# Load releases in a fused linear-attention and feed-forward kernel: fewer warm-up matmuls, weight and chunk loads tied to products

## The chip, the cores and the metric

The kernel runs on one core of one Trainium2 chip. The metric is the device time of one execution in microseconds; the figure given for a kernel is the median of its runs. Lower is better.

## The reference, cut to what matters

There are 4 batches, 8 heads, 768 positions and a head width of 64. The first half is linear attention with a decay per head, worked in blocks; the second half is a feed-forward layer with a "snake" activation over the 3072 tokens that come out of it.

```python
intra = einsum(q_block, k_block) * Dmask          # decay inside the block
out   = einsum(intra, v_block) + einsum(q_block * lam_pow, state)
state = lam_block * state + einsum(k_block * rev_pow, v_block)
...
h = x @ w_in                                      # 3072x512 by 512x2048
g = h + sin(alpha * h)**2 / (alpha + 1e-9)
y = g @ w_out                                     # 2048x512
```

## The kernel before, in words

**Attention steps.** Tokens are handled in 24 steps. A pair of batches, a block of 128 positions and a half of the heads make one step `s`; two steps share one load `d` (`d = s // 2`), so there are 12 loads each of q, k and v. q and k are cast to bf16 by their transfers[...]; v arrives as f32. `load(d, x)` (L298) issues two transfers, one for each batch of the pair; with `by_step=True` it issues four, one for each batch and half of the heads, so that a step can start on half of the data. For each step, `sec()` (L433) puts up to three pieces on TensorE (PE): the transposes of q and k (`t=`, L444), the scores (`s=`, L453) and the outputs together with the new state (`o=`, L466, L476, L489). Behind them, `prep_v` (L416, instruction L423) scales v by a decay table and casts it, `put_S` (L559) masks the scores on VectorE (DVE), and `put_O` (L571) writes the result transposed into `xT` (L581, DVE), copies the state `Zs` (L591 on ScalarE, called ACT, or L604 on GpSimd, called POOL) and keeps the running state `Zacc` (L586, L602). A step `o` needs its scaled v, its masked scores and the `Zs` of step `o-2`.

**Chunks.** Four steps give one chunk `c` of 512 tokens; there are six chunks. For each chunk, 16 groups `grp_A(c, m)` (L632, matmuls L640) form the first product, 128 columns of `w_in` each. A group is four matmuls of 128x512, and after it come a sine on ACT (L644), a square on whichever engine would end first (L649 to L653) and one combining instruction on DVE (L654) into `gT`. The second product is `grp_B(c, s4, m4)` (L669, matmuls L677): four 128-token tiles in four steps of four matmuls each. A finished tile is copied out by ACT (L684) and stored by two transfers on the SP queue (L690). "GEMM1 of chunk 1" below means the 16 groups `grp_A(1, 0..15)`; "the second product of chunk 0" means the `grp_B(0, ...)` that run just before them, with the attention steps 4 to 7 between them.

**Weights.** `w_in` comes in four blocks of four column groups (`w1_block`, L405, issue at L408) and `w_out` in four blocks (`w2_block`, L411, issue at L413), all cast to bf16 on the POOL queue.

**What sets the order.** Nothing in the program is issued in the order in which it is written. `Program.add` (L86) is a planner: each operation has an assumed duration, and `place` and `probe` (L65, L75) put it at the earliest time at which its inputs are ready and its engine has a gap. PE and SP keep the written order (they only have a `free` time); DVE, ACT and POOL can be back-filled. A transfer is planned from its issue cost (`ISSUE`, L35), one shared transfer rate (`RATE`), a start delay (`BEGIN`) and an end delay (`DONE`), L36, L107 to L114. A load on POOL is never placed before the load that was recorded ahead of it (`self.issued`, L109), but otherwise it goes as early as its buffer allows. The instructions are then emitted sorted by planned start (L117), with semaphore waits where one engine needs another. On the chip, each engine's queue runs strictly in this order. So the planned durations decide orders and engine choices (`fastest`, L284), and the real durations decide the time. An `after=` list adds dependencies by hand.

**The start.** L715 to L760 write the first four steps by hand. `idle_pe(32)` (L379) runs 32 matmuls on a zeroed tile; nothing reads them. The POOL queue gets, in this order, the loads of k, q for `d=0` and `d=1`, small constants, eight transfers for v (`d=0` and `d=1`, `by_step`), the first block of `w_in`, a small constant (L353), the four `prep_v` of steps 0 to 3, and the other three blocks of `w_in`. The first group of GEMM1 needs `xT` of steps 0 to 3.

**The loads of later chunks.** `ISSUE_A0`, `ISSUE_B0` and `ISSUE_A1` (L788 to L790) say after which group a load is recorded, not when it is issued. A load of chunk 2 (`d=4`, `d=5`) has a free buffer long before it is recorded, so the planner can back-fill it behind the load recorded before it. `ahead` (L764) records the `prep_v` of later steps and the loads `d` from 6 on.

Of the kernel before, what the change touches and what calls it, by code (L numbers as in the profile page):

```python
# [27 lines left out]
class Program:  # L28
# [4 lines left out]

    ENGINES = ("PE", "DVE", "ACT", "POOL", "SP")
    ISSUE = {"SP": 0.66, "POOL": 0.75, "ACT": 0.66}  # L35
    HOP, RATE, BEGIN, DONE = 0.1, 190e3, 1.6, 1.0  # L36

    def __init__(self):
        self.ops = []
# [46 lines left out]
    def add(self, eng, fn, dur, reads=(), writes=(), slot=None, nbytes=0, after=()):  # L86
        op = Op(eng, fn, dur, len(self.ops))
        self.ops.append(op)
        op.deps = self.deps_of(reads, writes) | set(after)
        for b in reads:  # L90
            if b.startswith("b."):
                op.deps.update(r for r in self.readers.get(b, ()) if r.eng != eng)
        for b in reads:
            self.readers.setdefault(b, []).append(op)
        for b in writes:
            self.writer[b] = op
            self.readers[b] = []
        op.nbytes = nbytes
        t = self.ready(eng, op.deps)
        if slot is None:  # L100
            op.start = self.place(eng, t, dur)
            op.end = op.start + dur
            return op
        op.slot = slot
        self.slots[slot] = self.slots.get(slot, 0) + 1
        op.kslot = self.slots[slot]
        issue = self.ISSUE[eng] * (0.6 if 10000 < nbytes < 100000 and eng == "POOL" else 1)  # L107
        op.start = self.place(eng, max(t, self.issued[eng]), issue)
        self.issued[eng] = op.start  # L109
        if nbytes < 10000:  # L110
            op.end = op.start + 2.9
        else:
            self.dma_free = max(self.dma_free, op.start + self.BEGIN) + nbytes / self.RATE
            op.end = self.dma_free + self.DONE  # L114
        return op
# [72 lines left out]
def bass_lightning_attn__then__act_snake_kernel(  # L188
# [10 lines left out]
    B, H, S, D = q.shape  # L199
# [20 lines left out]
    with es:  # L220
# [50 lines left out]
        P = Program()  # L271
# [26 lines left out]
        def load(d, x, after=(), by_step=False, eng=None):  # L298
            pair, n = d // NB, d % NB
            r = d % RL  # L300
            src, dst = {"k": (k, k2), "q": (q, q2), "v": (v, v32)}[x]
            ops = []
            for h0, h1 in ((0, HS), (HS, H)) if by_step else ((0, H),):
                for u in range(2):
                    a = bass.AP(src.tensor, ((2 * pair + u) * H + h0) * S * D + n * BL * D,
                                [[2 * D, 64], [S * D, h1 - h0], [1, 2 * D]])
                    keys = [f"{x}.{r}.{u}.{h // HS}" for h in range(h0, h1, HS)]
                    op = rec(eng or ("SP" if x == "v" else "POOL"),
                             lambda e, u=u, a=a, h0=h0, h1=h1: e.dma_start(dst[r][half(u), h0:h1, :], a), 0,  # L309
                             writes=keys, slot=f"{x}{r}{h0 if by_step else ''}{'p' if eng else ''}",  # L310
                             nbytes=(216500 if x == "v" and eng is None else 166000) * (h1 - h0) // H, after=after)
                ops.append(op)
            return ops if by_step else op

# [398 lines left out]
                        reads=[f"ol.{z}"], slot=f"ol{z}{t}", nbytes=64 * 1024)  # L713

        load(0, "k")  # L715
        q0 = load(0, "q")
        consts()
        idle_pe(32)
        iotas()
        consts3()  # L720
        load(1, "k")
# [2 lines left out]
        sec(t=0, tb=(0, 1), t_engs=("DVE",))  # L724
        sec(t=1, tb=(2, 3), t_engs=("ACT",))
        consts2()
        load(0, "v", by_step=True, eng="POOL")
        load(1, "v", by_step=True, eng="POOL")
        w1_block(0, 4)
        identf_op()  # L730
        decay_table(0, 2)
        sec(s=0, sb_=4)
        sec(t=2, tb=(0, 1), t_engs=("DVE",))
        sec(s=1, sb_=6)
        sec(t=3, tb=(2, 3), t_engs=("ACT",))
        decay_table(2, NB)
        prep_v(0, ("POOL",))
        prep_v(1, ("POOL",))
        sec(s=2, sb_=0)
        zl = []  # L740
        s3 = sec(s=3, sb_=2, via=True, later=True)
        sec(o=0, ob=4, z_late=zl)
        s3()
        prep_v(2, ("POOL",))
        prep_v(3, ("POOL",))
        sec(o=1, ob=6, z_late=zl)
        w1_block(4, 4)
        w1_block(8, 4)
        w1_block(12, 4)
        o2 = sec(o=2, ob=0, later=True)  # L750
# [27 lines left out]
            b = pick_bank(range(4)) if t is not None else 0  # L778
            return sec(t=t, o=o, s=s, tb=(b, b), peek=peek, x_first=i % 4 == 3)

        def loads(*what):
            for x, d in what:
                if x == "w":
                    w2_block(4 * d, 4)
                else:
                    load(d, x, eng="POOL" if d < 4 else None)

        ISSUE_A0 = {0: [("w", 0)], 2: [("k", 2)], 4: [("q", 2)], 6: [("w", 1)], 9: [("k", 3)], 12: [("q", 3)]}  # L788
        ISSUE_B0 = {0: [("v", 2), ("w", 2)], 2: [("v", 3), ("w", 3)], 8: [("k", 4)], 10: [("q", 4)]}
        ISSUE_A1 = {0: [("v", 4)], 1: [("k", 5)], 3: [("q", 5)], 4: [("v", 5)]}  # L790
        AHEAD_A1 = {8: 8, 11: 9, 14: 10}
        LAST_B0 = {1: (2, 3), 3: (3, 3)}
        every, low = range(8), range(4)
# [5 lines left out]
        SQ = {3: "ACT", 6: "DVE", 8: "ACT", 11: "DVE", 13: "ACT"}  # L799
        for c in range(NCH):  # L800
            for m in range(NM):
                grp_A(c, m, every if m < 12 else range(2, 4) if m == 15 and c else range(4, 8),
                      (SQ.get(m, "POOL"),) if c > 1 else ("POOL", "ACT", "DVE"))
                if c < 2:
                    loads(*(ISSUE_A0, ISSUE_A1)[c].get(m, ()))
                if c == 1 and m in AHEAD_A1:
                    ahead(AHEAD_A1[m])
                if c == 1 and m in LAST_B0:
# [58 lines left out]
```

## Time and profile before

| What | Value |
|---|---|
| median of 6 runs | 230.0 us (228.82 to 232.35) |
| the profiled execution, its own time | 229.39 us |
| its span from the first to the last instruction | 227.2 us |
| PE busy in the span | 207.5 us, 91% |
| DVE, ACT, POOL busy | 141.8, 125.0, 121.8 us |
| mean granted clock of PE | 0.960 |
| first group of GEMM1 of chunk 0 | from about 21.6 us |
| second product of chunk 0, with steps 4 to 7 | about 37 to 59.6 us |
| GEMM1 of chunk 1 | about 59.6 to 76 us |

All times inside the span count from its start. "PEld" is the loading of a stationary operand, which runs beside PE. In lists of waits, "<-issue" means that an engine stood still although nothing that the profile shows held it. In the list of transfers, q0 is the queue that POOL issues to, q1 the one that SP issues to, and q8 carries instructions to the engines.

### The profile page before, as it was taken

The page shows a single profiled execution, that of the slowest core. Times are in us where ns is not written, and L with a number is a line of the kernel's source. Part 1 is how long each engine was busy: PE and PEld are TensorE (multiplying, and loading weights), DVE is VectorE, ACT ScalarE, POOL GpSimd, SP SyncE. Part 2 cuts the span into 40 slices and gives each one's busy share as a digit, 9 for nine tenths or more (in the row PEclk, how much of TensorE's full clock was granted, in tenths as well). Part 3 has the DMA queues.
Part 4 walks back from the last instruction along what each step waited for, and adds up shares of the span by engine and source line. Part 5 has one row for each costly group of instructions (what it writes and reads, how often), then busy time and mean ns, then how long its engine had stood idle before and what let it go on. Part 6 is the DMA issues. An engine that isn't in the chain of part 4 may idle for free.

```text
span 227.2 us, 6426 instructions
## 1 busy us (share of the span) xinstructions
PE 207.5 (91%) x2800; PEld 109.9 (48%) x2833; DVE 141.8 (62%) x201; ACT 125.0 (55%) x194; POOL 121.8 (54%) x160
## 2 busy tenths in 40 slices
PE   6377999986999899999999999999999999999994
PEld 5255444453444455544455544455544554444453
DVE  2768599464579955658747487855478664378400
ACT  4835699130499734577636577533677432568130
POOL 8997999325603516685626587533364500555300
PEclk9655899999999999999999999999999999999999
DMA  7988999999999606990509942503200204102043
GB/s 67 154 194 124 206 179 193 243 196 144 130 187 283 127 3 93 194 137 0 133 8 120 234 48 23 139 3 88 58 0 3 48 3 95 46 0 48 1 92 92
DMA packets 42923, 23.49 MB, mean 103 GB/s; under 512 B 26880, under 2 KB 39440, under 8 KB 42896
## 3 DMA queue, kind: packets, MB, share of 16 engines
q0 software_dynamic: 30272, 12.59, 44.2%
q1 hardware_dynamic: 12368, 10.42, 18.8%
q8 instruction: 22, 0.36, 0.6%
q10 hardware_dynamic: 256, 0.08, 0.2%
q14 instruction: 5, 0.04, 0.1%
HBM read 27.28 MB, written 6.29 MB: 148 GB/s over the span
## 4 chain that ended last, share of the span: by engine, by line
PE 81%; DVE 7%; POOL 6%; issue 4%; ACT 1%; POOLq 0%
PE PS L640 33%; PE PS L677 32%; PE PS L444 5%; DVE gT L654 3%; PE PS L466 3%; PE PS L476 3%; PE PS L453 2%; POOL v L309 2%; PE PS L704 2%; PE PS L489 1%; DVE u L652 1%; POOL k L309 1%; POOL q L309 1%; DVE S_m L568 1%; DVE xT L581 1%
## 5 line engine op out<-in xcount | busy, mean ns | idle before, releaser
L640 PE MATMUL PS<-xT,w 128*128 128x512 bf16 x376 | 86.8, 383 | 1.3 <-DVE Zacc L602 1.0
L677 PE MATMUL PS<-w,gT 128*128 128x512 bf16 x343 | 82.0, 379 | 3.8 <-issue 3.6
L654 DVE SCALAR_TENSOR_TENSOR gT<-u,r_sb,PS 128x512 bf16<-128x512 bf16 x96 | 69.7, 746 | 24.7 <-POOL u L652 21.8
L644 ACT ACTIVATE t<-PS,alpha_sb 128x512 bf16<-128x512 f32 x96 | 63.4, 682 | 21.5 <-PE PS L640 21.3
L652 POOL TENSOR_TENSOR u<-t 128x512 bf16<-128x512 bf16 x44 | 45.3, 1049 | 31.5 <-ACT t L644 31.4
L640 PEld LDWEIGHTS PS<-xT,w 128*128 128x128 bf16 x384 | 37.3, 99 | 47.7 <-issue 2.5
L677 PEld LDWEIGHTS PS<-w,gT 128*128 128x128 bf16 x368 | 33.9, 98 | 39.6
L568 DVE TENSOR_TENSOR S_m<-PS,mask 128x1024 bf16<-128x1024 f32 x23 | 28.0, 1222 | 22.8 <-PE PS L453 22.8
L623 ACT COPY qkT<-PS 128x1024 bf16<-128x1024 bf16 x21 | 21.2, 1011 | 29.4 <-PE PS L476 18.9
L423 POOL TENSOR_TENSOR v<-v,Lv 128x512 bf16<-128x512 f32 x20 | 20.9, 1059 | 30.1 <-DMA v<-in_v_dram 15.9
L684 ACT COPY osb<-PS 128x512 f32<-128x512 f32 x23 | 13.5, 585 | 31.4 <-PE PS L677 31.4
L581 DVE TENSOR_TENSOR xT<-PS,Xt 128x512 bf16<-128x512 f32 x24 | 16.3, 684 | 12.9 <-PE PS L476 11.9
L309 POOL DMA_DIRECT2D k<-in_k_dram x24 | 17.3, 745 | 8.7 <-PE PS L476 4.9
L444 PE MATMUL PS<-ident,q 64*64 64x64 bf16 x384 | 14.3, 205 | 6.2 <-DMA q<-in_q_dram 5.1
L651 ACT ACTIVATE u<-t 128x512 bf16<-128x512 bf16 x28 | 17.6, 630 | 1.4
L604 POOL CAST Zs<-Zacc 128x256 bf16<-128x256 f32 x16 | 6.8, 428 | 20.0 <-DVE Zacc L602 20.0
L444 PEld LDWEIGHTS PS<-ident,q 64*64 64x64 bf16 x384 | 9.7, 114 | 15.9 <-issue 11.0
L309 POOL DMA_DIRECT2D q<-in_q_dram x24 | 17.1, 743 | 0.0
L652 DVE TENSOR_TENSOR u<-t 128x512 bf16<-128x512 bf16 x24 | 14.2, 592 | 3.2 <-ACT t L644 3.2
L476 PE MATMUL PS<-qkT,Zs 64*64 64x128 bf16 x160 | 15.6, 232 | 0.4
L466 PE MATMUL PS<-S_m,v 64*64 64x128 bf16 x384 | 14.2, 235 | 1.1 <-POOL v L423 0.7
L444 PE MATMUL PS<-ident,k 64*64 64x64 bf16 x384 | 13.5, 200 | 0.0
(50 smaller groups left out, 131.8 us busy)
## 6 DMA issues: line engine op xcount, KB each, us to landing
out_dram<-osb SPq DMA_DIRECT2D x46, 128.0 KB, 3.0
v<-in_v_dram SPq DMA_DIRECT2D x16, 256.0 KB, 6.4
k<-in_k_dram POOLq DMA_DIRECT2D x24, 128.0 KB, 5.7
q<-in_q_dram POOLq DMA_DIRECT2D x24, 128.0 KB, 6.5
w<-in_moe_w_in_dram POOLq DMA_DIRECT2D x4, 512.0 KB, 7.4
w<-in_moe_w_out_dram POOLq DMA_DIRECT2D x4, 512.0 KB, 13.1
v<-in_v_dram POOLq DMA_DIRECT2D x8, 128.0 KB, 3.5
v<-in_v_dram POOLq DMA_DIRECT2D x4, 256.0 KB, 13.9
```

The lines of the kernel that those rows point to most:

```text
L309: lambda e, u=u, a=a, h0=h0, h1=h1: e.dma_start(dst[r][half(u), h0:h1, :], a), 0,
L423: rec(eng, lambda e: e.tensor_tensor(v2[c][:, :, :], src, L_b, ALU.mult), dur, reads=reads, writes=writes)
L444: last = e.transpose(dst, part((q2, k2)[x], t, u, h, tt), ident[half(u), half(u)])
L466: return e.matmul(dst, v2[o % RC][half(u), hid(h, tj), :], S_m[o % RS][half(u), h % 2 ^ u, h // 2, tj, :], start=start, stop=True, skip_gr ...
L476: return e.matmul(dst, Zs[(o - 2) % 3][half(r), u, h // 2, :], qkT[o % RQ][half(r), u, 0, h // 2, :], start=start, stop=True, skip_group_c ...
L568: rec("DVE", lambda e: e.tensor_tensor(s_out, s_in, mask_b, ALU.mult), 1.25, reads=keys_s + ["mask.0", "mask.1"], writes=[f"S_m.{s % RS}"])
L623: rec(eng, lambda e: (e.copy if eng == "ACT" else e.tensor_copy)(to, ti), dur, reads=keys_t, writes=[f"qkT.{j}"])
L640: last = e.matmul(PS[:, i, :], w1[:, kc, 128 * m:128 * (m + 1)], xT[x][:, kc, :], start=(kc == 0), stop=(kc == NKC - 1))
L644: rec("ACT", lambda e: e.activation(t16[tt][:, :], PS[:, i, :], ACTF.Sin, scale=alpha_sb[:, m:m + 1]), 0.7, reads=bk(i) + ["alpha"], write ...
L652: return e.tensor_tensor(u16[tt][:, :], t16[tt][:, :], t16[tt][:, :], ALU.mult)
L654: rec("DVE", lambda e: e.scalar_tensor_tensor(out=gT[g][:, m, :], in0=u16[tt][:, :], scalar=r_sb[:, m:m + 1], in1=PS[:, i, :], op0=ALU.mul ...
L677: last = e.matmul(PS[:, bank, :], gT[g][:, m, 128 * s4:128 * (s4 + 1)], w2[:, m, :], start=(m == 0), stop=(m == NM - 1))
```

## The change

- The planner's constants: `BEGIN` 1.6 to 1.5, `DONE` 1.0 to 1.2, the issue cost of mid-sized POOL transfers, and the assumed sizes of q, k and v transfers.
- 16 zero matmuls in place of 32.
- v for `d=1` is loaded by two transfers in place of four.
- Scores of step 1 are recorded ahead of the transposes of step 2; outputs of step 0 are recorded ahead of the scores of step 3.
- The second block of `w_in` is recorded right after the outputs of step 0, and waits for them (`after=[P.ops[-1]]`, the PE piece of `o=0`); the scalings of v for steps 2 and 3 are recorded behind it. The third and fourth block stay behind those.
- The loads of k and q for `d=4` move from the second product of chunk 0 to GEMM1 of chunk 1. Every load recorded in GEMM1 of chunk 1 (k, q, v of `d=4` and `d=5`) waits for the PE piece of the group after which it is recorded.

```diff
-    HOP, RATE, BEGIN, DONE = 0.1, 190e3, 1.6, 1.0
+    HOP, RATE, BEGIN, DONE = 0.1, 190e3, 1.5, 1.2
...
-        issue = self.ISSUE[eng] * (0.6 if 10000 < nbytes < 100000 and eng == "POOL" else 1)
+        issue = self.ISSUE[eng] * (0.85 if 10000 < nbytes < 100000 and eng == "POOL" else 1)
...
-                             nbytes=(216500 if x == "v" and eng is None else 166000) * (h1 - h0) // H, after=after)
+                             nbytes=(187000 if d < 2 else 150000) if x != "v" else 216500 // (2 if by_step else 1), after=after)
...
-        idle_pe(32)
+        idle_pe(16)
...
-        load(0, "v", by_step=True, eng="POOL")
-        load(1, "v", by_step=True, eng="POOL")
+        load(0, "v", eng="POOL", by_step=True)
+        load(1, "v", eng="POOL")
         w1_block(0, 4)
         identf_op()
         decay_table(0, 2)
         sec(s=0, sb_=4)
+        sec(s=1, sb_=6)
         sec(t=2, tb=(0, 1), t_engs=("DVE",))
-        sec(s=1, sb_=6)
         sec(t=3, tb=(2, 3), t_engs=("ACT",))
         decay_table(2, NB)
         prep_v(0, ("POOL",))
         prep_v(1, ("POOL",))
+        zl = []
         sec(s=2, sb_=0)
-        zl = []
-        s3 = sec(s=3, sb_=2, via=True, later=True)
-        sec(o=0, ob=4, z_late=zl)
-        s3()
+        o0 = sec(o=0, ob=4, z_late=zl, later=True)
+        w1_block(4, 4, after=[P.ops[-1]])
+        sec(s=3, sb_=2, via=True)
+        o0()
+        sec(o=1, ob=6, z_late=zl)
         prep_v(2, ("POOL",))
         prep_v(3, ("POOL",))
-        sec(o=1, ob=6, z_late=zl)
-        w1_block(4, 4)
         w1_block(8, 4)
         w1_block(12, 4)
...
-        def loads(*what):
+        def loads(*what, after=()):
...
-                    load(d, x, eng="POOL" if d < 4 else None)
+                    load(d, x, eng="POOL" if d < 4 else None, after=after)
...
-        ISSUE_B0 = {0: [("v", 2), ("w", 2)], 2: [("v", 3), ("w", 3)], 8: [("k", 4)], 10: [("q", 4)]}
-        ISSUE_A1 = {0: [("v", 4)], 1: [("k", 5)], 3: [("q", 5)], 4: [("v", 5)]}
+        ISSUE_B0 = {0: [("v", 2), ("w", 2)], 2: [("v", 3), ("w", 3)]}
+        ISSUE_A1 = {1: [("k", 4)], 2: [("q", 4), ("v", 4)], 4: [("k", 5)], 5: [("q", 5), ("v", 5)]}
...
-                grp_A(c, m, every if m < 12 else range(2, 4) if m == 15 and c else range(4, 8),
+                op = grp_A(c, m, every if m < 12 else range(2, 4) if m == 15 and c else range(4, 8),
...
-                    loads(*(ISSUE_A0, ISSUE_A1)[c].get(m, ()))
+                    loads(*(ISSUE_A0, ISSUE_A1)[c].get(m, ()), after=[op] if c else [])
```

## The prediction

> **What bounds the kernel now.** I read the 40 slices of the page first, then the chain of work that ended last over the start, then the gaps of PE in the list in order of time, and last the transfer queues around the largest gap.
>
> ```profile
> PE   6377999986999899999999999999999999999994
> PEclk9655899999999999999999999999999999999999
> DMA  7988999999999606990509942503200204102043
> ```
>
> After the fourth slice (22 us) PE is full, but for the ninth and tenth (45 to 57 us) and, less, the fourteenth. So a microsecond is to be had in the first 22 us, in the 50s, or nowhere: elsewhere an earlier load finds PE busy anyway. The start, by the chain:
>
> ```profile
> 9.25 4.17 POOL v L309 x7
> ...
> 13.51 0.87 POOL w L408
> ...
> 14.48 1.03 POOL v L423
> 15.56 0.64 PE PS L466 x16
> ...
> 20.88 0.69 DVE xT L581
> ```
>
> POOL's queue sets it: eight v transfers, the first `w_in` block, a constant, then the scaling that step 0's outputs wait for. The end of the start is the `xT` of step 3 at 21.57 us; GEMM1 follows. The hole in the 50s, by PE's list in order of time:
>
> ```profile
> 51.52 0.22 PE L476 MATMUL PS<-qkT,Zs 64*64 64x128 bf16 x2
> 53.37 0.33 PE L489 MATMUL PS<-v,k 64*64 64x64 bf16 x12 [1.63 <-issue]
> ```
>
> PE stops 1.63 us in the middle of one emitted piece, step 5's outputs, where no semaphore wait can stand.[...] What is left is that its instructions were not there. Two views speak for that. Busy times with instruction counts, from zero to the end of the hole and from zero to 47.07 us:
>
> ```profile
> 0.00:53.36 53.36, 41.29 (x722) 25.01 (x729) 35.48 (x53) 29.60 (x50) 41.29 (x66) 0.84 1.20 173
> 0.00:47.07 47.07, 37.21 (x596) 22.46 (x602) 31.27 (x48) 28.59 (x49) 39.46 (x64) 0.82 1.15 171
> ```
>
> PE and PEld together: 1451 against 1198, 253 apart. The page's queue q8 has 22 instruction packets of 0.36 MB for 5633 PE and PEld instructions, 256 per packet of 16 KB. So the block that was missing at 53.37 could be asked for when the one before the last was used up, at about 47.07. The queues at the one packet near it (window 50.9 to 51.1 us):
>
> ```profile
> q0 software_dynamic: 141, 0.04, 178.0%
> q8 instruction: 1, 0.02, 29.6%
> ```
>
> It left only at 51.00, 3.9 us after 47.07, while POOL's transfers (q0) filled the 16 engines. At about 80 us, with q0 empty, the same step two blocks on took 0.9 us, from 79.98 to 80.85. What fills q0 then:
>
> ```profile
> 33.54 0.91 POOL L413 DMA_DIRECT2D w<-in_moe_w_out_dram  x1
> 34.30 1.53 POOL L309 DMA_DIRECT2D k<-in_k_dram  x2
> 35.65 1.53 POOL L309 DMA_DIRECT2D q<-in_q_dram  x2
> 36.99 1.56 POOL L309 DMA_DIRECT2D k<-in_k_dram  x2
> 38.32 1.58 POOL L309 DMA_DIRECT2D q<-in_q_dram  x2
> ```
>
> These k and q are `d=4` and `d=5`, chunk 2, back-filled to 34 us although nothing needs them before 76 us. Their landing times in the transfer view are 16.7 to 17.4 us (51.0 to 55.7); the last `w_out` block lands at 33.54 + 17.1 = 50.6.
>
> **The change, part by part.**
>
> *Zero matmuls.* The 32 take 3.47 us (1.17 to 4.64). The Trainium skill (TensorE: Matmul & The Clock Gate, "Part 1: The HAM clock gate") says that some 3.4 us of sustained work release the clock; 16 matmuls, 1.73 us, would by that not release it, and the rule speaks against halving them. If the release reached the start's work, 9.36 us of PE at half rate, losing it could cost up to 4.7 us (half of it). But the rows say that it reaches nothing:
>
> ```profile
> 4.64:8.20 3.56, 0.00 (x1) 0.00 (x1) 2.61 (x5) 2.10 (x6) 3.56 (x7) 0.94 1.34 127
> 8.20:21.60 13.40, 9.36 (x337) 7.57 (x337) 10.07 (x13) 8.16 (x14) 12.53 (x19) 0.50 0.95 159
> ```
>
> PE idles until q lands at 8.2, and from there its clock is 0.50 with all 32 in place. I take 0. A side effect: 32 fewer PE instructions (16 and their weight loads) move each block end 32 instructions later in the program.
>
> *v in six transfers.* Eight cost 4.99 us on POOL, 0.62 each. Now 4 x 0.62 + 2 x 0.74 (row of `d=2`: 1.48 a pair) = 3.98: `w_in`, the constant and the first scalings come 1.01 us earlier, step 0's outputs at 14.55 in place of 15.56. Scaling 2 now needs all of `d=1`; the last of its small transfers landed at 12.9 + 3.3 = 16.2, and the new ones are issued by 12.6, so it is there at about 16.
>
> *Second `w_in` block.* It waits for step 0's outputs (to 15.41), is issued at 15.5 for 0.80 us, and behind it in POOL's queue stand scalings 2 and 3, then blocks three and four. So scaling 2 ends at 17.33 (17.49 before), scaling 3 at 18.33 (18.49). Of the 1.01 us, 0.85 is spent here. Step 3's masking is the other gate of step 3:
>
> ```profile
> 17.10 1.94 DVE L565 TENSOR_TENSOR S_m<-S_raw,mask 128x1024 bf16<-128x1024 bf16 x1
> ```
>
> It ends at 19.04, 0.55 after POOL's last scaling, though begun at 17.10. Step 3's scores now run after step 0's outputs (15.4 to 16.0), ACT copies them in 1.01, so it begins at 17.05, again under scaling 3: it ends at 18.9. Then 2.5 us to GEMM1 as before. The start gains 0.15 us. Bounds: 1.0 gained if the masking gets in ahead of scaling 3 and everything moves by POOL's 1.01; 0.6 lost if `d=1` lands that much later. The early block itself lands before 22, where it was needed at 27: hidden. If GEMM1 ever waited for it, its issue at 15.5 in place of 18.44 would be worth 2.9 us.
>
> *Step 1's scores first.* They fit into PE's wait for q of `d=1` (10.8 to 11.85): 0. Their masking (1.22) delays a DVE copy by 0.26, hidden behind the scalings. *Planner constants.* They reorder, they cost nothing alone. ACT's sine table (1.28 + 0.20 at 20.07) fits into a planned gap behind the decay tables, as the planner now has the copy of step 3 later; ACT is not in the chain there: 0.
>
> *Chunk 2's loads.* Eight POOL issues leave 34 to 40 us, where POOL then waits idle: 0. The loads of `d=6`, `d=7` move with them, since no load passes the one ahead. The fetch for the block that ends in the hole is now asked for at 47.5 and its code needed at 52.4 (32 instructions on, without the hole). From the last `w_out` block q0 is empty, at 50.6 or earlier: the `w_in` blocks start sooner, into the 18 to 20 us slot where only 53 GB/s moved, which takes up to 2 us off the queue, so at about 49. Fetch 49.0, packet 0.95, and from the packet to PE's restart before 53.37 - 51.95 = 1.42: code at 51.4, or at 53.0 with 50.6. That is a stall of 0 to 0.6 us in place of 1.63; I take 0.3, a gain of 1.3. Bounds: 0 (the fetch's lag is that of `w_out`, not of chunk 2) and 1.63. The skill's Runtime: NRT & Kernel Launch, "Instruction fetch mechanics", has the fetch of 256 instructions mostly hidden; by that rule the hole is something else, the gain 0 and the sum 229.4. The row, 253 instructions and a late packet, is nearer; I go by it.
>
> In GEMM1 of chunk 1 the eight issues (1.36 to 1.53 a pair) stand on POOL from 61.5 to 68.6, each pair held until a group ends. Behind them are the scalings of steps 8 and 9 (70.5 before) and nothing else. POOL was idle from 63 to 70.5, and that hides 5.7 us of issue; without it the scalings would slip toward 82, where step 8 is used. SP: v of `d=4` moves behind two stores (63.34, 0.92 each), from 61.5 to about 65.2, v of `d=5` from 67.1 to 68.8, `d=6` to 70.7. Landing in 7 us, v4 is there at 72 and scaled by 74; needed at 82.3: hidden. k, q of `d=4` have 12 us to 76: hidden. But transfers crowd 62 to 84 now, 4.2 MB and the stores at 175 to 250 GB/s, 22 us. Two blocks fetched at 80 and 86 have 5.3 and 4.4 us: lost 0 to 1.6, taken 0.2, since the queue thins by then.
>
> *Sum* against the profiled execution: 229.39 - 0.15 - 1.3 + 0.2 = 228.1. The median of the runs is 0.6 above that execution: **228.7**.
>
> **Rivals.**
>
> *The hole only moves.* q0 is still full of `w_out` at 47.5, or the later crowd holds up the fetch at 86 as it did at 47. Then 230.0 - 0.15 to + 0.3: 229.8 to 230.3. For: 3.6 us of lag at 44.37 already, with chunk 2 hardly moving. Against: the packet left within 0.4 us of `w_out`'s landing.
>
> *The start gives all of its 1.01.* For: POOL leads the chain from 8.7 to 15.5. Against: the masking's 1.94. 228.7 - 0.9 = 227.8.
>
> *Slower: a scaling on DVE waits for v of `d=6`.* The planner gives a scaling to the engine that ends first, and at step 12's scaling it now sees this v later than before, when DVE has a gap, at about 82. DVE's queue is in order: behind it is the masking of step 9 (83.50). From a landing at 82.8 on, each microsecond of lateness goes to PE. Issued at 70.7 and landing in 6.6 to 7.2 us it comes at 78; with the longest v landing of the trace, 15.9, at 86.6, and 3.8 are lost: 228.7 + 3.8 = 232.5.
>
> **How the numbers follow.** Hole filled, start unchanged 0.52 (228.7, its own range 227.5 to 229.7); hole moves 0.20; start gains 0.15; slower 0.13. About 1% is what a measurement of this kernel can tell from no change: below 227.7, above 232.3. Faster: half of the start's case, a quarter of the first: 0.22. Slower: the DVE case and a tenth of the moved hole: 0.15. Same 0.63. Range 226.8 to 231.5.
>
> **What would show it.** Right: chunk 2's k and q at 61 to 69 us; no PE gap over 0.6 in 45 to 57; GEMM1 from 21.3 to 21.7; clock 0.5 from 8 us on as before. Wrong: GEMM1 from 20.7 (the start counted), a gap in 85 to 91 (fetch), an idle DVE at 82 to 87 ahead of L423 (v6), PE's clock at half for longer than 25 us.

## The result, and the profile after

| | kernel before | kernel after |
|---|---|---|
| median of the runs | 230.52 us (70 runs) | 231.47 us (228.75 to 234.18, 33 runs) |
| ratio after/before | | 1.003, 95% interval 1.0007 to 1.0054 |
| the profiled execution, its own time | 229.39 us | 230.43 us |
| its span | 227.17 us | 228.22 us |

The change makes the kernel a little slower; the forecast was 228.7 us, 0.6% faster. (Ratios here and below leave disturbed runs out; in group C of the experiments that leaves only 16 of 75 runs of the kernel before, so there the medians of all runs are read as well.)

The two profiled executions differ by 1.05 us of span. Taking from each trace the start of the first group of GEMM1 of chunk 0, of the second product of chunk 0, and of GEMM1 of chunks 1 and 2 gives the place of each part:

| stage | before | after | difference |
|---|---|---|---|
| to GEMM1 of chunk 0 | 21.62 | 22.46 | +0.84 |
| GEMM1 of chunk 0 | 15.19 | 16.01 | +0.82 |
| second product of chunk 0 and steps 4 to 7 | 22.74 | 21.54 | -1.20 |
| GEMM1 and second product of chunk 1 | 35.43 | 35.97 | +0.54 |
| the rest | 132.19 | 132.24 | +0.05 |

So the expected gain is there, in the third stage, and three others give it back. (How much of that belongs to the change, and how much to this pair of executions, is told below.) The page of the changed kernel, 40 slices again:

```profile
PE   3465999998999998999999999999999999999994
PEclk9999999999999999999999999999999999999999
DMA  6999999960399999990418952604200204101043
```

The row PEclk does not mean full speed in the start. The first clock record of this trace is at 26.56 us, and a stretch without a record reads 1.00; the spacing of the matmuls shows half rate until then (the first two groups of GEMM1 take 1.26 and 1.71 us, as in the kernel before, and 0.86 later).

The dip of PE in the ninth and tenth slice is gone (9 and 8 instead of 8 and 6). The new one is small, in the sixteenth slice (86 to 91 us), where the kernel before had a 9. In DMA, the ninth to eleventh slice have emptied (9, 9, 9 to 6, 0, 3) and the fourteenth and fifteenth, 74 to 86 us, have filled up (6 and 0 to 9 and 9). The gaps of PE in the order of time that are longer than 0.4 us, behind the first group of GEMM1:

```profile
54.46 1.90 PE L677 MATMUL PS<-w,gT 128*128 128x512 bf16 x7 [0.41 <-issue]
...
86.83 0.21 PE L444 MATMUL PS<-ident,k 64*64 64x64 bf16 x1 [0.77 <-issue]
```

The hole that was 1.63 us at 53.37 is 0.41 us, behind step 5's outputs in place of in the middle of them. The one at 86.83 is new, again in the middle of an emitted piece, where no semaphore wait can stand.

**The second late block.** PE and PEld had used up a block of 256 instructions at about 80.1 us, and the next packet of q8 left at 84.33. The transfer queues around it (84.2 to 84.5 us; packets, MB, and the summed time of the packets as a share of the 16 engines, which can be above 100%):

```profile
q0 software_dynamic: 192, 0.05, 161.1%
q8 instruction: 1, 0.02, 18.6%
```

4.2 us from request to packet, with q0 full: the lag that was 3.9 us at 47 to 51 in the kernel before. In the kernel before, the transfers were done by then. Busy time and DMA share in three stretches, before and then after (the last three columns are granted clock, DMA share and GB/s):

```profile
80.00:85.00 5.00, 4.68 (x133) 2.90 (x130) 2.72 (x3) 2.03 (x2) 1.04 (x1) 1.00 0.01 3
85.00:90.00 5.00, 4.58 (x129) 2.57 (x130) 3.40 (x6) 2.19 (x3) 2.87 (x6) 1.00 0.45 76
```

```profile
80.00:85.00 5.00, 4.68 (x130) 2.83 (x126) 2.79 (x3) 2.02 (x2) 2.68 (x3) 1.00 1.51 205
85.00:90.00 5.00, 3.77 (x99) 2.27 (x99) 2.68 (x6) 2.18 (x3) 1.93 (x4) 1.00 0.98 128
```

PE loses 0.81 us of busy time in the second stretch (4.58 to 3.77).

**The start.** POOL's list in order of time:

```profile
13.69 2.04 POOL L423 TENSOR_TENSOR v<-v,Lv 128x512 bf16<-128x512 f32 x2 [0.27 <-DMA v<-in_v_dram]
15.98 0.80 POOL L408 DMA_DIRECT2D w<-in_moe_w_in_dram  x1 [0.25 <-PE PS L489]
17.43 2.32 POOL L423 TENSOR_TENSOR v<-v,Lv 128x512 bf16<-128x512 f32 x2 [0.66 <-DMA v<-in_v_dram]
19.71 1.55 POOL L408 DMA_DIRECT2D w<-in_moe_w_in_dram  x2
```

POOL came to the scaling of step 2 at 16.8 us and waited 0.66 us for v of `d=1`. The masking of step 3, which the prediction took for the second gate, began in that wait and ended at 17.85, long before POOL's last scaling (19.75):

```profile
17.16 0.69 DVE L565 TENSOR_TENSOR S_m<-S_raw,mask 128x1024 bf16<-128x1024 bf16 x1 [0.75 <-ACT S_raw L564]
```

It had been 1.94 us long when POOL was scaling as it began. Here it began first, and POOL's scaling of step 2, begun within it, took 1.32 us in place of 1.03. So in this execution v, not the masking, set the end of the start.

**GEMM1 of chunk 0.** The kernel before has an uninterrupted run of groups to its end. The changed one, where PE's list breaks:

```profile
28.80 6.21 PE L640 MATMUL PS<-xT,w 128*128 128x512 bf16 x28
35.22 3.63 PE L640 MATMUL PS<-xT,w 128*128 128x512 bf16 x15 [0.21 <-DVE gT L654]
```

A matmul waits for DVE's combining instruction of an earlier group. What the line L640 waited for between 33 and 38 us, and who waited for L654 in that time (us, times):

```profile
  DVE gT L654: 0.8, 3
...
  PEld PS L640: 0.6, 2
  PE PS L640: 0.2, 1
```

From the starts of the groups' first weight loads, groups 11 to 14 are 1.42, 0.68, 1.08 and 0.76 us long, 3.94 together, where the kernel before has four times 0.86, 3.44: 0.50 us. The rest of that stage's 0.82 is mostly the clock: PE's full rate came 4.10 us after the stage's start (26.56) in place of 3.24 (24.86), and until then a group takes 1.71 us in place of 0.86, which is some 0.4 us.

The banks are the planner's doing. `pick_bank` (L281) takes the PSUM bank that is free first in the plan. Groups 0 to 11 may use all eight, groups 12 to 15 only four (banks 4 to 7). The two plans give groups 0 to 15 these banks:

```
before: 5 6 7 0 1 4 2 3 5 6 7 0 4 5 6 7
after:  5 6 7 4 0 1 2 3 5 6 7 4 5 6 7 4
```

In the new plan the sine table (L389) stands earlier in the start, at 10.96 in place of 17.96 us of planned time. The copy that reads bank 4 no longer stands behind it, and bank 4 looks free before bank 0 (20.59 and 21.23; in the plan of before 19.76 and 19.58). So group 3 takes bank 4, and group 11 again. The new constants alone (e8) and the new start alone (e7) give the same banks. Group 12 then has to take bank 5, which group 8 left only four groups ago; before, it had bank 4, untouched since group 5.

### The profile page after: what moved, and what is told of

Same layout as the page of the kernel before. It is cut to its first block, busy times and chain, and to the rows that moved or that the text cites. A ratio compares the mean times of both kernels' runs of the same rounds, so it can differ in the third digit from the quotient of the medians.

```text
span 228.2 us, 6391 instructions
## 1 busy us (share of the span) xinstructions
PE 206.2 (90%) x2784; PEld 107.8 (47%) x2817; DVE 139.8 (61%) x201; ACT 124.9 (55%) x194; POOL 121.0 (53%) x158
## 4 chain that ended last, share of the span: by engine, by line
PE 84%; DVE 4%; POOL 4%; issue 4%; DMA 2%; ACT 1%; POOLq 0%; DVEq 0%
PE PS L640 34%; PE PS L677 34%; PE PS L444 5%; PE PS L466 3%; PE PS L476 3%; PE PS L453 3%; DVE gT L654 2%; DMA v<-in_v_dram 2%; PE PS L704 2%; POOL k L309 1%; POOL q L309 1%; PE PS L489 1%; DVE xT L581 1%; DVE S_m L568 1%; POOL v L423 0%
## 5 line engine op out<-in xcount | busy, mean ns | idle before, releaser
L640 PE MATMUL PS<-xT,w 128*128 128x512 bf16 x376 | 87.5, 385 | 1.6 <-DVE Zacc L602 1.0
L677 PE MATMUL PS<-w,gT 128*128 128x512 bf16 x343 | 81.9, 379 | 4.2 <-issue 4.1
L654 DVE SCALAR_TENSOR_TENSOR gT<-u,r_sb,PS 128x512 bf16<-128x512 bf16 x96 | 69.8, 746 | 24.8 <-POOL u L652 21.5
L640 PEld LDWEIGHTS PS<-xT,w 128*128 128x128 bf16 x384 | 37.2, 99 | 48.6 <-issue 3.7
L677 PEld LDWEIGHTS PS<-w,gT 128*128 128x128 bf16 x368 | 33.9, 98 | 40.1 <-issue 0.6
L423 POOL TENSOR_TENSOR v<-v,Lv 128x512 bf16<-128x512 f32 x20 | 21.0, 1063 | 24.6 <-DMA v<-in_v_dram 15.5
L444 PE MATMUL PS<-ident,q 64*64 64x64 bf16 x384 | 14.3, 205 | 5.7 <-POOL ident L316 5.0
L444 PEld LDWEIGHTS PS<-ident,q 64*64 64x64 bf16 x384 | 9.6, 114 | 15.5 <-issue 7.2
L652 DVE TENSOR_TENSOR u<-t 128x512 bf16<-128x512 bf16 x24 | 13.4, 557 | 4.1 <-ACT t L644 4.1
L444 PE MATMUL PS<-ident,k 64*64 64x64 bf16 x384 | 13.7, 200 | 0.8 <-issue 0.8
```

What stands on the lines that cost most here:

```text
L423: rec(eng, lambda e: e.tensor_tensor(v2[c][:, :, :], src, L_b, ALU.mult), dur, reads=reads, writes=writes)
L444: last = e.transpose(dst, part((q2, k2)[x], t, u, h, tt), ident[half(u), half(u)])
L640: last = e.matmul(PS[:, i, :], w1[:, kc, 128 * m:128 * (m + 1)], xT[x][:, kc, :], start=(kc == 0), stop=(kc == NKC - 1))
L652: return e.tensor_tensor(u16[tt][:, :], t16[tt][:, :], t16[tt][:, :], ALU.mult)
L654: rec("DVE", lambda e: e.scalar_tensor_tensor(out=gT[g][:, m, :], in0=u16[tt][:, :], scalar=r_sb[:, m:m + 1], in1=PS[:, i, :], op0=ALU.mul ...
L677: last = e.matmul(PS[:, bank, :], gT[g][:, m, 128 * s4:128 * (s4 + 1)], w2[:, m, :], start=(m == 0), stop=(m == NM - 1))
```

## The experiments

Four groups of kernels, each measured side by side with the kernel before on one chip.

| | kernel | median, us | before beside it | ratio, 95% interval |
|---|---|---|---|---|
| A | e1_loads_only | 230.39 | 231.06 | 0.9977, 0.9946 to 1.0008 |
| A | e2_start_only | 233.03 | 231.06 | 1.0084, 1.0038 to 1.0131 |
| A | e3_v_by_step | 232.57 | 231.06 | 1.0029, 0.9991 to 1.0066 |
| A | e4_idle16 | 230.79 | 231.06 | 0.9987, 0.9955 to 1.0019 |
| B | e5_loads_thinned | 228.83 | 231.07 | 0.9905, 0.9876 to 0.9935 |
| B | e6_change_thinned | 229.38 | 231.07 | 0.9966, 0.9941 to 0.9990 |
| B | e7_start_old_planner | 232.75 | 231.07 | 1.0097, 1.0058 to 1.0136 |
| B | e8_planner_only | 233.20 | 231.07 | 1.0062, 1.0026 to 1.0097 |
| C | e9_change_old_banks | 230.60 | 231.79 | 0.9989, 0.9954 to 1.0025 |
| C | e10_thinned_old_banks | 228.82 | 231.79 | 0.9913, 0.9881 to 0.9945 |
| C | e11_old_start_new_banks | 228.71 | 231.79 | 0.9977, 0.9942 to 1.0011 |
| C | e12_planner_two_undone | 231.95 | 231.79 | 1.0125, 1.0088 to 1.0162 |
| D | e15_thinned_base | 228.70 | 230.88 | 0.9939, 0.9910 to 0.9968 |
| D | e13_four_banks | 228.94 | 230.88 | 0.9962, 0.9927 to 0.9998 |
| D | e14_three_banks | 230.92 | 230.88 | 1.0050, 1.0021 to 1.0080 |
| D | e16_change_beside_base | 231.51 | 230.88 | 1.0030, 0.9999 to 1.0060 |

In group C, e10 and e11 have the same median and ratios 0.6% apart: the ratios of that group carry no finer than that.

### Which part of the change costs: loads alone, start alone

e1 is the kernel before with only the moved loads of chunk 2:

```diff
-                    load(d, x, eng="POOL" if d < 4 else None)
+                    load(d, x, eng="POOL" if d < 4 else None, after=after)
...
-        ISSUE_A1 = {0: [("v", 4)], 1: [("k", 5)], 3: [("q", 5)], 4: [("v", 5)]}
+        ISSUE_A1 = {1: [("k", 4)], 2: [("q", 4), ("v", 4)], 4: [("k", 5)], 5: [("q", 5), ("v", 5)]}
```

> Only the loads of chunk 2 are moved and tied to groups; the start, the 32 zero matmuls and the planner's constants stay. Theory A (the start lost what the loads won): the start's GEMM1 begins at 21.5 to 21.8 us as before, the hole of 1.63 us in step 5's outputs is gone or under 0.5, a new one of up to 0.8 us stands at 84 to 87 us, and the time is 0.2 to 0.5% below the kernel before (ratio 0.995 to 0.998). Rival B (the moved loads themselves cost, by the crowd of transfers after 62 us): ratio 1.001 to 1.004, the same as the whole change.

The hole of the 50s is gone: PE passes the instruction ahead of which it stood at 54.65 us without a stop. Another stands at 50.13 (the second line has busy times and counts up to it):

```profile
50.13 0.31 PE L444 MATMUL PS<-ident,k 64*64 64x64 bf16 x7 [0.68 <-issue]
0.00:50.12 50.12, 37.86 (x597) 22.65 (x602) 31.21 (x48) 28.86 (x49) 35.11 (x57) 0.80 1.13 169
```

1199 instructions of PE and PEld lie ahead of it, where 1451 lay ahead of the hole of the kernel before. So it is one block earlier, at the count of 1198 that the kernel before passed at 47.07 without such a hole. A new hole of 0.85 us stands at 87.54, as in the changed kernel. Ratio 0.9977, and its interval reaches 1: the loads alone gain little, since they give back at 50 and 87 most of what they gain at 53.

e2 is the changed kernel with the loads where they were:

```diff
-        ISSUE_B0 = {0: [("v", 2), ("w", 2)], 2: [("v", 3), ("w", 3)]}
+        ISSUE_B0 = {0: [("v", 2), ("w", 2)], 2: [("v", 3), ("w", 3)], 8: [("k", 4)], 10: [("q", 4)]}
```

> The whole change without the moved loads: start, constants and 16 zero matmuls only. Theory A: v for d=1 lands at about 17.4 us, scaling 2 is late, GEMM1 begins at 22.3 to 22.6 us, the hole in the 50s is still there (1.0 to 1.7 us), ratio 1.003 to 1.007. Rival B: ratio 0.998 to 1.001.

1.0084: without the moved loads, the rest of the change is a loss. The hole stays (1.78 us at 55.47) and the uneven groups of GEMM1 are there. But GEMM1 begins at 21.77 in its profile, earlier than expected, and the scaling of step 2 at 16.68 without a wait, so a late start is not what that execution shows.

### v of d=1 in four transfers

```diff
-        load(1, "v", eng="POOL")
+        load(1, "v", eng="POOL", by_step=True)
```

> The whole change, but v for d=1 again comes in four transfers. Theory A (scaling 2 waited for all of d=1): its half is there by 16.3, scaling 2 starts at 17.0 to 17.6 us right behind the second w_in block without a wait for a transfer, GEMM1 begins at 21.5 to 22.0, ratio 0.996 to 1.000. Rival C (the second w_in block in front of the scalings is what is late, not the transfer): GEMM1 stays at 22.3 or later, ratio 1.001 to 1.005.

The scaling of step 2 now waits for no transfer, but POOL comes to it later, behind four issues, so it starts at 17.60 in place of 17.43:

```profile
16.78 0.80 POOL L408 DMA_DIRECT2D w<-in_moe_w_in_dram  x1 [0.25 <-PE PS L489]
17.60 2.06 POOL L423 TENSOR_TENSOR v<-v,Lv 128x512 bf16<-128x512 f32 x2
```

Issue cost and landing stand so close behind each other that the one released by the change is taken by the other; GEMM1 begins at 22.79. The same profile, of an execution of 234.0 us, shows the largest hole at the second place, and behind it the clock at half:

```profile
88.85 0.21 PE L444 MATMUL PS<-ident,k 64*64 64x64 bf16 x1 [2.08 <-issue]
```

```profile
PEclk9999999999999997999999999999999999999999
```

The "7" is 3.4 us at half rate from 90.2 us.

### Zero matmuls, and whether the hole is an instruction block

e4 is the kernel before with 16 zero matmuls:

```diff
-        idle_pe(32)
+        idle_pe(16)
```

> The kernel before with 16 zero matmuls in place of 32. If the zero matmuls have no use: ratio 0.998 to 1.002. If the hole in the 50s is a late block of instructions, it moves 32 TensorE and weight-load instructions on: from the middle of step 5's outputs to the first L677 matmul behind them, with 1.2 to 1.7 us. If the hole belongs to the outputs (a bank, the data), it stays ahead of L489. If the clock at the start depends on them: clock above 0.5 somewhere from 8 to 21 us before, not with 16.

```profile
55.23 1.90 PE L677 MATMUL PS<-w,gT 128*128 128x512 bf16 x7 [1.94 <-issue]
```

The hole moved from L489 inside step 5's outputs to the first L677 behind them. That is 32 PE and PEld instructions further on in the program, just what the 16 matmuls and their 16 weight loads take away ahead of it. A wait for data would have stayed at its instruction; a block end moves. The time is the same (0.9987). For the clock the recorded values can't be compared (e4's first record is at 26.02 us, so its rows read 1.00 in the start), but the spacing of the matmuls is the same in both. 16 transposes of L444 start within 0.19 to 0.21 us, where the row of the kernel before has 0.50, and GEMM1's first two groups take 1.26 and 1.71 us.

### Fewer transfers where the second block is fetched

e5 is e1, and e6 the changed kernel, with the loads of `d=7` held behind a later PE piece (on the chip they go from 90.6 us on in e5 and 89.5 in e6, where the expectation had 86) and those of `d=8` behind the first group of GEMM1 of chunk 2:

```diff
-                if p % 2 and nl[0] < 2 * NB:
+                if p % 2 and p != 11 and nl[0] < 2 * NB:
+                    held_by = [o for o in P.ops if o.eng == "PE"][-1:] if nl[0] == 7 else []
...
-                        load(nl[0], x)
+                        load(nl[0], x, after=held_by)
...
+                if c == 2 and m == 0:
+                    for x in "kqv":
+                        load(nl[0], x, after=[op])
+                    nl[0] += 1
```

> The kernel before with chunk 2's loads moved, and in addition the loads of d=7 are held back to about 86 us and those of d=8 to the first group of chunk 2's GEMM1, so that 0.77 MB less runs between 70 and 85 us. If the hole near 87 us is an instruction block held up by that crowd: transfers end by about 81 us, no hole over 0.4 near 87, GEMM1 of chunk 1 to that of chunk 2 takes 35.0 to 35.6 us (36.6 with the loads moved alone), and the time is 0.4 to 1.0% below the kernel before (ratio 0.990 to 0.996). If the hole comes from elsewhere: it stays at 0.7 to 2 us and the ratio at 0.997 to 1.000.

> The whole change with the same thinning. If the start of the change costs nothing by itself: ratio 0.990 to 0.997, the same as without it. If the start costs 0.4% or more: ratio 0.997 to 1.002.

Neither has a PE gap over 0.4 us behind the start. The same stretches of e5, then of e6:

```profile
80.00:85.00 5.00, 4.62 (x147) 3.10 (x149) 2.92 (x4) 2.00 (x2) 1.04 (x1) 1.00 0.96 120
85.00:90.00 5.00, 4.58 (x104) 2.58 (x104) 4.12 (x7) 2.21 (x4) 0.83 (x2) 1.00 0.25 56
```

```profile
80.00:85.00 5.00, 4.65 (x102) 2.47 (x102) 3.25 (x4) 1.79 (x3) 2.08 (x2) 1.00 0.57 58
85.00:90.00 5.00, 4.70 (x146) 3.08 (x150) 2.19 (x4) 2.11 (x3) 1.04 (x3) 1.00 0.34 80
```

With a DMA share of 0.96 or 0.57 in place of 1.51, PE is busy 4.58 and 4.70 us in the second stretch, against 3.77. e5 at 0.9905 beats both kernels, e6 at 0.9966 the changed one. The moved loads with the thinning are a gain of 0.6 to 1% (e5 again, as e15: 0.9939), once the traffic that they pushed on is out of the way of the next block. What the thinning would give the kernel before, without the moved loads, was not tried.

All traces together say the same. Take as the lag the time from the moment at which PE and PEld had used up the block before the last to the next packet of q8. For the block of the 50s it is 3.8 to 4.6 us in the six kernels with the old loads (the kernel before, e2, e4, e7, e8, e12) and 0.9 to 3.1 in all with moved ones. For the block asked for at about 80 us it is 0.6 to 0.9 us with the old loads, 4.2 to 5.6 with moved ones (the changed kernel, e1, e3, e9, e16), and 1.4 to 2.7 with moved and thinned ones (e5, e6, e10, e11, e13 to e15).

### The start without the constants, the constants without the start

e7 takes the change's start (the section from the first loads to the third `w_in` block) into the kernel before; e8 takes its constants alone:

```diff
-    HOP, RATE, BEGIN, DONE = 0.1, 190e3, 1.6, 1.0
+    HOP, RATE, BEGIN, DONE = 0.1, 190e3, 1.5, 1.2
...
-        issue = self.ISSUE[eng] * (0.6 if 10000 < nbytes < 100000 and eng == "POOL" else 1)
+        issue = self.ISSUE[eng] * (0.85 if 10000 < nbytes < 100000 and eng == "POOL" else 1)
...
-                             nbytes=(216500 if x == "v" and eng is None else 166000) * (h1 - h0) // H, after=after)
+                             nbytes=(187000 if d < 2 else 150000) if x != "v" else 216500 // (2 if by_step else 1), after=after)
```

> Only the new start (16 zero matmuls, v in two transfers, second w_in block behind step 0's outputs, the new order) with the old planner's constants; from GEMM1 of chunk 0 on every engine's order is that of before. If the start itself is slow: GEMM1 begins at 22.0 us or later, ratio 1.003 to 1.007. If the start is neutral and the start-only kernel of before lost its time to a scaling that the new constants put on DVE: ratio 0.998 to 1.002.

> Only the planner's constants and assumed sizes are changed. They move the sine table ahead in ACT's queue and the scaling of step 12 from POOL to DVE, where it waits for v of d=6. If that scaling is what costs in the start-only kernel: DVE waits at L423 for a transfer near 78 to 82 us in some executions, ratio 1.003 to 1.008. If not: 0.998 to 1.002.

Both are slower (1.0097 and 1.0062), and both have group lengths of 1.43, 0.68, 1.08, 0.76 (e8's) in GEMM1 of chunk 0: each alone brings the plan to the new banks. e8 also puts the scaling of step 12 on DVE, as the prediction's third rival had it:

```profile
82.15 0.68 DVE L423 TENSOR_TENSOR v<-v,Lv 128x512 bf16<-128x512 f32 x1
83.59 1.23 DVE L568 TENSOR_TENSOR S_m<-PS,mask 128x1024 bf16<-128x1024 f32 x1 [0.75 <-PE PS L453]
```

There is no wait ahead of it: v of `d=6` was there, and the next masking waits for its scores only. So that is not what makes e8 slower. The banks' 0.50 us is not all of it either: e7 and e8 lose 2.2 and 1.4 us by their ratios. Where the rest goes is open.

### The banks

e9 is the changed kernel, e10 is e6, with the old banks; e11 is e5 with the new ones. On every engine the order of instructions stays as it was.

```diff
-                op = grp_A(c, m, every if m < 12 else range(2, 4) if m == 15 and c else range(4, 8),
+                op = grp_A(c, m, [(5, 6, 7, 0, 1, 4, 2, 3, 5, 6, 7, 0, 4, 5, 6, 7)[m]] if c == 0 else every if m < 12 else range(2, 4) if m == 15 and c else range(4, 8),
```

> The changed kernel with the PSUM banks of the sixteen groups of chunk 0's GEMM1 forced to those of the kernel before (5, 6, 7, 0, 1, 4, 2, 3, 5, 6, 7, 0, 4, 5, 6, 7 in place of 5, 6, 7, 4, 0, 1, 2, 3, 5, 6, 7, 4, 5, 6, 7, 4); every engine's order of instructions stays as it is. Bank theory (the new banks cost 0.4 to 0.5 us, because group 12 takes a bank that only group 8 has just left): groups 11 to 14 of chunk 0 start 0.86 us apart each, the second product of chunk 0 begins 0.4 to 0.5 us earlier for the same clock in GEMM1, span 227.7, ratio to before about 1.001. Rival (the uneven spacing comes from the ScalarE and VectorE work in the start and stays): spacing still 1.4, 0.7, 1.1, 0.8, ratio 1.003 as in the changed kernel. The hole near 87 us (0.77 us) should stay in both.

> The changed kernel with the loads of d=7 and d=8 held back and with the old banks in chunk 0's GEMM1. If the two costs (instruction blocks behind the crowd of transfers, and the banks) are apart and both are the change's only losses, they add: 0.9966 less 0.2 per cent for the banks, 0.9945, at most 0.99 if the new start gives anything; no hole over 0.4 us after 22 us. Rival: the gap between this kernel thinned (0.9966) and the kernel before with moved and thinned loads (0.9905) is the new start's own, then this stays at 0.996 to 0.997.

> The reverse: the kernel before with the moved and thinned loads (0.9905 against the kernel before), old start and old constants, but the new kernel's banks forced on chunk 0's GEMM1; orders stay. Bank theory: 0.4 to 0.5 us slower than without them, 0.992 to 0.993, spacing of groups 11 to 14 becomes 1.4, 0.7, 1.1, 0.8. Rival (banks cost nothing alone): 0.9905 and an even 0.86 spacing.

PE's list over GEMM1 of chunk 0, in e9 and then in e11:

```profile
28.67 9.66 PE L640 MATMUL PS<-xT,w 128*128 128x512 bf16 x44
38.16 2.11 PE L677 MATMUL PS<-w,gT 128*128 128x512 bf16 x9
```

```profile
28.71 5.56 PE L640 MATMUL PS<-xT,w 128*128 128x512 bf16 x25
34.49 3.69 PE L640 MATMUL PS<-xT,w 128*128 128x512 bf16 x16 [0.22 <-DVE gT L654]
```

The wait goes with the banks, in both directions: e9's groups are 0.86 us each, e11's 1.43, 0.70, 1.12, 0.76 (0.57 us over four times 0.86). In whole runs it is less plain. e9 is below the kernel before (0.9989; medians 230.60 against 231.79), where the change itself is above it, and its hole at 86.37 stays, 0.74 us. e10 has the lowest time of the changed kernels, although a hole of 0.69 us stands at 55.13 in its profile, where none over 0.4 was expected. But e11 is no slower than e5 was (medians 228.71 and 228.83). 0.5 us is 0.2%, less than what two groups of measurements differ by, so what the banks cost in whole runs is not shown.

e12 is e8 with the old banks and the scaling of step 12 forced on POOL:

```diff
-                prep_v(p)
+                prep_v(p, ("POOL",) if p == 12 else ("POOL", "DVE"))
```

> The kernel before with the planner's new constants only (1.0062 against the kernel before), and in it the old banks in chunk 0's GEMM1 and the scaling of v for step 12 forced on GpSimd, so that two of the three choices that the constants changed are undone; the early sine table on ScalarE stays. If banks and that scaling are what the constants cost: 1.000 to 1.002. If the table itself, or a shift in time that lets transfers meet instruction blocks, costs the rest: 1.004 to 1.006.

Its groups are even again. The medians of all runs are 231.95 and 231.79, no difference, where e8 stood 2.1 us above; the ratio of group C says 1.0125. The two don't agree, and this run settles nothing of the time.

Group D therefore makes the suspected wait more frequent, on one base. e15 is e5 again; e13 (the first added line) and e14 (the second) use four banks and three banks in turn in chunk 0's GEMM1; e16 is the changed kernel beside them.

```diff
-                op = grp_A(c, m, every if m < 12 else range(2, 4) if m == 15 and c else range(4, 8),
+                op = grp_A(c, m, [(5, 6, 7, 4)[m % 4]] if c == 0 else every if m < 12 else range(2, 4) if m == 15 and c else range(4, 8),
...
+                op = grp_A(c, m, [(5, 6, 7)[m % 3]] if c == 0 else every if m < 12 else range(2, 4) if m == 15 and c else range(4, 8),
```

> The kernel before with the moved and thinned loads once more, as the base for the two bank kernels of this call: 0.990, even spacing of 0.86 us in chunk 0's GEMM1.

> That base with only the banks 5, 6, 7, 4 in turn for all sixteen groups of chunk 0's GEMM1; orders stay. In the changed kernel each group that takes a bank only four groups old waits once in four for its VectorE combine, about 0.55 us, less what the next groups win back. Bank theory: such a wait at groups 4, 8 and 12 in place of 12 alone, so 1.0 to 1.5 us over the base (0.4 to 0.65 per cent), 0.995 to 0.997, and PE's wait for gT (L654) shows in the trace. Rival (the waits are made up by a later slack of PE): 0.990 as the base.

> That base with three banks 5, 6, 7 in turn; orders stay. A group's bank is then taken again only after sine, square and combine of the group three back; from the changed kernel's groups these take 0.68, 0.56 to 1.05 and 0.75 us behind its 0.86, some 3 to 3.4 us, so a group every 1.0 to 1.15 us in place of 0.86. Bank theory: 2 to 4 us over the base, 1.0 to 1.01. Rival: under 1 us.

> The changed kernel once more, beside the thinned base: 1.003, so 1.2 to 1.3 per cent (2.9 us) above the base: banks 0.5 us, hole at 87 us 0.8, and the rest from the start and from half-clock windows behind late instruction blocks in a third of the runs.

With three banks a group takes 1.06 to 1.14 us in place of 0.86, and the kernel is 2.2 us slower than its base (230.92 against 228.70): a bank that comes back too soon costs what the theory says. With four, the forecast of 1.0 to 1.5 us was a miss. The lengths are 1.18, 0.68, 1.08, 0.70 over and over from group 7 on, 3.64 for four groups in place of 3.44, and the second product begins 15.83 us after GEMM1 in place of 15.51; the median is 0.24 us above the base. A likely reason is in DVE: its combining instructions end on average 0.91 to 0.92 us apart in the base and in e13 alike, and the last ends 18.73 and 18.59 us after GEMM1's start. With eight banks PE runs ahead of that pace at 0.86 us a group; with four it can't. What is lost is that lead, bit by bit in e13 (0.2 us for each four groups) or all at once in the changed kernel, where PE meets the four banks late. It is not 0.5 us at each fourth group, as I had it.

e16 against e15 is the clearest figure for what the change leaves on the table: 231.51 against 228.70, beside each other on one chip.

## Why the prediction was wrong, point by point

The forecast was 1.3 us down, from 230.0 to 228.7; the median stands 0.95 us up, at 231.47 against 230.52. The gain at the hole of the 50s came. What failed are two terms of the sum: the cost of the crowd of transfers at the next late block, taken as 0.2 us, and that of the planner's constants, taken as 0.

- **The hole in the 50s is a late block of instructions.** Right: e4 moved it by exactly the 32 instructions taken out ahead of it, and the moved loads shrank it. The block could be asked for at 49.2, and its packet left 2.5 us later in place of 3.9. Forecast stall 0.3, measured 0.41 us; gain 1.22 us of the 1.3. The trace goes here against the rule of the Trainium skill (Runtime: NRT & Kernel Launch, "Instruction fetch mechanics") that such fetches are mostly hidden, by which the gain would have been nothing.
- **16 zero matmuls cost nothing.** Right: e4, 0.9987. With 32 the trace has a full-rate record from 4.38 to 7.79 us, with 16 none before 26.02, but the work begins at 8.23 and 8.03 and has the same spacing in both. The sign "clock 0.5 from 8 us on" can't be read from the row of the changed kernel, which has no record there; the spacing of its matmuls agrees with it.
- **The start gains 0.15 us.** In size it can't be told: the first group begins between 21.36 and 23.28 us in the executions of kernels with the old start and the old constants, between 21.77 and 23.12 in those with the new start. The reasoning failed in one term. v of `d=1` was to be there "at about 16"; POOL waited for it to 17.43 (in e6, e9 and e16 to 17.16, 17.42 and 16.79, in e2 not at all), and e3 showed that smaller transfers only give the wait back to the issue queue. The 1.94 us masking that was thought to be the gate was so long because POOL was scaling when it began.
- **"Planner constants. They reorder, they cost nothing alone."** This failed. I asked what they do to the order of the instructions and looked at engine and queue only. The plan also hands out the PSUM banks, and the sine table, which I let move for nothing, changed whose bank is free first: 0.50 us in GEMM1 of chunk 0. e9 and e11 show that the wait comes with the banks alone, though not that whole runs get longer by it. That the table's place is what tips the choice was read from the plan, not tried by itself, and the new start alone moves the table too.
- **"Lost 0 to 1.6, taken 0.2, since the queue thins by then."** This is the term that was mis-sized. The prediction had counted the loads of `d=4` to `d=7` into the crowd and let them end at 84 us, with a thin queue at the fetch of 80. They landed until 89.0; the DMA share was 1.51 from 80 to 85 and 0.98 from 85 to 90 us. The block that could be asked for at 80.1 came 4.2 us later, PE stood 0.77 us (2.08 in e3), and the stage lost 0.54 us against the kernel before, which waits 0.47 us for DVE there (at 79.32). The fetch behind it, at 86.8, took 1.15 us and held up nothing. In whole runs the crowd costs more than in this pair: e6, which takes it out of the changed kernel, is at 0.9966 in place of 1.003, 1.5 us, and the hole at 87 goes. The prediction had named this mechanism in its first rival, for the fetch at 86, and gave it a fifth.
- **The rival in which a scaling on DVE waits for v of `d=6`.** It didn't come: the scaling of step 12 stayed on POOL at 81.23, and in e8, where it is on DVE, DVE waits for no transfer.
- **Two slips that change nothing.** The fetch at 80 us is three blocks on from the one at 47, not two; and the shares of the chance of "faster" add up to 0.205, not 0.22.

With the measured terms the sum against the profiled execution is 229.39 + 0.84 (start) + 0.50 (banks) + 0.32 (mostly the clock, whose release came later after the start) - 1.20 + 0.54 + 0.05 = 230.4, the time of the changed kernel's execution. Of these, the start and the clock's release lie within what executions of one start differ by, so they aren't put down to the change. Without them the pair differs by -0.1 us, so this pair alone does not show the loss of the medians (230.52 to 231.47). The crowd at 80 us, by e6, is the largest part that an experiment shows; and 13 of 34 executions of the changed kernel are longer by about 3 us at a lower mean clock, which no single profile shows (last section). What is left open is whether the new start itself costs anything: e2 and e7, with the hole of the 50s in place, are at 1.0084 and 1.0097; e10 (0.9913) beside e5 and e15 (0.9905 and 0.9939) shows no such cost with the two others taken out.

## What to carry to other kernels

A transfer that is moved away from one late instruction block is moved toward another: count the instructions to the block ends around both places, before (e1) and behind, and look at the queue there, with every load that follows in the same queue, before calling the new place free. A planner's constants decide buffers and banks as well as orders; after such a change, compare which bank each product gets and how many products ago it was last used. And where an issue cost and a landing lie within some tenths of each other, removing one shows nothing.

## What the runs showed of the hardware that was not expected

- **Half-rate windows in mid-kernel.** In e3's profile, PE's clock fell to half for 3.4 us, 1.4 us after a gap of 2.08 us. Of the 34 executions of the changed kernel, 13 had a mean granted clock of 0.993 (median 233.5 us against 230.4 for the others); of the 22 of e16, 10 had 0.985 to 0.993 (233.5 against 229.9). That is one or two such windows (3.4 x 0.5 / 228 is 0.7%). A window takes at most 1.7 us, half of its length, so it is not all of the 3.1 to 3.6 us. Of 44 executions of e6 and e10, the changed kernel without the hole at 87 us, none had such a mean. But a hole is not enough: with one in the 50s, e2 (1.78 us) had it in 14 of 22 executions, e4 (1.94 us) in none. What brings the windows is open.
- **A full POOL queue holds back instructions.** A block of 16 KB took about 4 us from request to packet while POOL's transfers had a share of 1.6 to 1.8 of the engines, against 0.9 us with the queue empty. The time of the request is inferred from the count of instructions.
- **One masking, several durations.** L565 on DVE and a scaling on POOL (L423, else 1.03 to 1.07 us) stretch each other. Where POOL was scaling already, the masking took 1.94 us (the kernel before), up to 2.72 (e12). Where it began while POOL waited (the changed kernel, e6, e9), it took 0.69 us, and the scaling that began within it 1.32 to 1.49. In e14 and e15 it took 0.95 to 0.99 us, and the last scaling beside it 1.51 to 1.54.
